# Attention of the second pair of token blocks: two tiles to a TensorE run instead of one

## The chip, the cores and the metric

The kernel runs on one core of one Trainium2 chip. The metric is the time of one launch on the device, in microseconds (us). Five engines work side by side, each through its own queue in order: TensorE (PE, matmuls), VectorE (DVE), ScalarE (ACT), GpSimd (POOL), and SyncE (SP), which only issues DMAs. An engine that needs another's result waits on a semaphore, and everything behind it in its queue waits too.

## The reference, cut to what matters

Attention inside chunks of 64 tokens (8 heads of 64), then a mixture of four experts in which every token goes through every expert, weighted by its normalised probability:

```
scores = q_c @ k_c.T / 8            # per chunk of 64 tokens and head
attn   = exp(scores - max); attn = attn / (sum(attn) + 1e-9)
x      = (attn @ v_c) as 4608 x 512 tokens
p      = domain_probs / (sum + 1e-9)
out    = sum over e of p[:, e] * (relu(x @ w1[e]) @ w2[e])   # 512 -> 1024 -> 512
```

## The kernel before

The 4608 tokens are nine blocks of 512, and a block is four tiles of 128. The first block is worked alone, and the other eight as four pairs. For each pair the weights are gone through in eight passes (four experts, two halves of the hidden units each), numbered n = 8 to 15 for the first pair, 16 to 23 for the second and so on. Products are in split fp32 (a high and a low part, three matmuls for each product of two 128-blocks), and a product of two blocks by two is made by a scheme of seven products instead of eight.

A later pass is 28 **products** of six matmuls 128x512 each, in the written order `WOVEN`: `a1 g1 a2 g2 g6 a5 g5 a6 a3 g7 a7 g4 g3 a4 h1 h2 b1 b5 h6 b6 b3 h5 b7 h7 b2 b4 h4 h3`, counted from 0 (g3 is the 12th, b2 the 24th). The g and h products make hidden units of this pass, the a and b products turn those of the pass before into output. `a` and `b` share the three PSUM banks A1, B1, C1 (class `Outer`), `g` and `h` the banks A0, B0, C0 (class `LaterGroup`). In bank A1 a product is accumulated onto the last one: after a1, a6, a7 and a4, DVE adds the bank's content to an output sum in SBUF (`Outer.add`, L989, rows `acc<-A`). The next matmul into A1 has to wait for that add. So b1 waits for the add after a4, and a1 of the next pass for the add after b4. (In pass 9, where each output sum is begun, that first write is a copy on ACT.)

Beside the matmuls each pass makes the weights' parts for the other passes: half sums (L579, rows `xraw<-xraw`, DVE), high parts on ACT, low parts on POOL.

The attention of the next pair is worked in between. One tile's attention is: scores on PE (32 matmuls of 64x64 in the trace) into PSUM tile `psa`; on DVE the row maxima and their subtraction (`less_max`, L314 and L319); exponentials on ACT (L325); on DVE the **weights** (L328 row sums, L329, L331 inverses, L335 scaling into SBUF, L188 a transpose back into `psa`); on ACT five copies that place the transposed weights (L194, L204); and on PE the values (32 matmuls, L214). A list `at` gives for each position the work that is recorded behind that product; every engine's queue holds it in this recorded order.

For the third and fourth pair `attend_two` handles two tiles to one TensorE run: values of two tiles and scores of the next two, 128 small matmuls together. For the second pair, whose attention stands in passes 9 to 14, `attend` handles one tile to a run: values of tile t and scores of tile t+1, 64 small matmuls. The places are `EARLY` (weights behind the 6th product, placing behind the 9th, run behind the 11th) and `LATE` (17th, 20th, 23rd), and behind each run come the maxima. Passes 10, 12 and 14 have an early run, 11 and 13 an early and a late one, pass 9 the first scores and a late run. The values leave PSUM by ACT and are kept in DRAM (`x_kept`) until the second pair begins.

Of the kernel before, what the change touches and what calls it, by code (L numbers as in the profile page):

```python
# [31 lines left out]
def chunk_attention_moe(ctx: ExitStack, tc: tile.TileContext, qk, v, v0, dp, w1, w2, out):  # L32
# [85 lines left out]
    def a_load(t):  # L118
        s = st[t] = {}
        s["x"] = load.tile([P, 2, 2, HG, C], F32, name="qk_in")  # L120
        nc.sync.dma_start(out=s["x"], in_=qk[t].rearrange("g c d x h s -> (c d) g x h s"))

    def a_load_v(t, odd=(False, True)):
        s = st[t]
        if not odd[0]:
            s["v"] = load.tile([P, 2 * HG, C], F32, name="v_in")
        to, of = (
            a.rearrange("p (g i h) d -> p g i (h d)", g=2, i=2) for a in (s["v"], v[t - NT])
        )
        if not odd[0]:  # L130
            nc.sync.dma_start(out=to[:, :, 0], in_=of[:, :, 0])
        if odd[-1]:
            for half in range(2):
                rows, other = slice(half * C, (half + 1) * C), slice((1 - half) * C, (2 - half) * C)
                nc.sync.dma_start(out=to[rows, :, 1], in_=of[other, :, 1])

    def a_load_after(t):
        if (t + 1 - NT) % (PAIR * NT):
            a_load(t + 1)

    def quarters():

        for g in range(2):
# [8 lines left out]
    def blocks(i):  # L152

        return psa[:, :, i * HG * C : (i + 1) * HG * C].rearrange("p c (j k) -> p c j k", k=C)

    def a_scores(t):
        s = st[t]
        s["sc"] = blocks(0)
        for c, half, slot, head in quarters():
            q, k = (s["x"][of_half(c), head // HG, x, head % HG] for x in range(2))  # L160
            nc.tensor.matmul(s["sc"][of_half(half), c, slot], lhsT=q, rhs=k, start=True, stop=True)  # L161

    def a_less_max(t):
        less_max(st[t]["sc"])

# [4 lines left out]
        a_less_max(t)  # L170
        a_exps(t)

    def a_sums(t):
        z = psa[:, 0, HG * C : HG * C + 2 * HG].rearrange("p (c j) -> p c j", c=2)
        st[t]["r"] = inverse_sums(st[t]["sc"], z)

    def a_scale(t):

        s = st[t]
        s["e"] = att.tile([P, 2, HG, C], F32, name="e")  # L180
        scale(s["e"], s["sc"], s["r"])

    def a_weights(t):
        a_sums(t)
        a_scale(t)

    def a_transpose(t):
        nc.vector.transpose(st[t]["sc"], st[t]["e"])  # L188

    def a_place(t, name="pt", apart=False):  # L190

        s = st[t]
        s["pt"] = att.tile([P, 2, HG, C], F32, name=name)
        nc.scalar.copy(out=s["pt"], in_=s["sc"])  # L194
        if not apart:
            a_place_rest(t)

    def a_place_rest(t):

        s = st[t]  # L200
        for half in range(2):
            for i in range(2):
                here, there = (slice(half * C + k * B, half * C + (k + 1) * B) for k in (i, 1 - i))
                nc.scalar.copy(  # L204
                    out=s["pt"][there, :, :, i * B : (i + 1) * B],
                    in_=s["sc"][here, :, :, (1 - i) * B : (2 - i) * B],
                )

    def a_values(t):

        s = st.pop(t)
        av = blocks(1)
        for c, half, slot, head in quarters():
            nc.tensor.matmul(  # L214
                av[of_half(slot % 2), half, head // 2], lhsT=s["v"][of_half(half), head],
                rhs=s["pt"][of_half(half), c, slot], start=True, stop=True,
            )

    def a_copy(t):
        pair, i = divmod(t - NT, PAIR * NT)  # L220
        if pair == 1:
            tile_x = scratch[0][:, :SUB].rearrange("p (j q) -> p j q", j=NK)
        else:
            tile_x = of_tiles(pair, i, 1)[:, 0]
        to = tile_x.rearrange("p j (c q) -> p c j q", c=2)
        av = blocks(1)
        nc.scalar.copy(out=to[:, :, 0::2], in_=av[:, :, 0::2])
        nc.scalar.copy(out=to[:, :, 1::2], in_=av[:, ::-1, 1::2])
        if pair == 1:
            nc.sync.dma_start(out=x_kept[:, i], in_=tile_x)  # L230

    def x_tiles(pair):
        xraw[pair] = xpool.tile([P, PAIR * NT, NK, P], F32, name="xraw")
# [12 lines left out]
        nc.sync.dma_start(out=to, in_=qk[t].rearrange("g c d x h s -> (c d) g x h s"))  # L248

    def two_load_v(t, i, odd):  # L250
        if i and not odd:
            pair, j = divmod(t - NT, PAIR * NT)
            st[t]["v"] = of_tiles(pair, 7 if j == 7 else 5, 1)[:, 0].rearrange("p j (h d) -> p j h d", h=2)
        elif not odd:
            st[t]["v"] = load.tile([P, NK, 2, C], F32, name="v_in")
        to = st[t]["v"].rearrange("p (g i) h d -> p g i h d", i=2)
        of = v[t - NT].rearrange("p (g i h) d -> p g i h d", g=2, i=2)
        if not odd:
            nc.sync.dma_start(out=to[:, :, 0], in_=of[:, :, 0])
            return  # L260
        for half in range(2):
            rows, other = slice(half * C, (half + 1) * C), slice((1 - half) * C, (2 - half) * C)
            nc.sync.dma_start(out=to[rows, :, 1], in_=of[other, :, 1])
# [17 lines left out]
    def two_next(t, scores, banks=("B1", "C1")):  # L281
# [14 lines left out]
                two_scores(scores + i, i)  # L296
        if av:
            pair, j = divmod(t - NT, PAIR * NT)
            to = of_tiles(pair, j, 2).rearrange("p i j (c q) -> p i j c q", c=2)
            for half in range(2):  # L300
                for odd in range(2):
                    nc.scalar.copy(out=to[:, :, odd::2, half ^ odd], in_=av[half][:, :, odd::2])

    x_kept = dram.tile([P, PAIR * NT, NK, P], F32, name="x_kept")

    def x_back():
        x = x_tiles(1)
# [29 lines left out]
    def attention(pair):  # L337
# [14 lines left out]
        for t in range(first, last, 2):  # L352
# [14 lines left out]
                if i == 0:  # L367
                    loads(t + 1, 1)
            two_next(t, t + 2 if t + 2 < last else None, (None, None))

    def a_next(t, after):

        if t is not None:
            a_values(t)
        if after is not None:
            a_scores(after)

        if t is not None:
            a_copy(t)

    KEYS = {"a11": 0, "a12": 1, "a22": 2, "s1": 3, "s2": 4, "s3": 5, "s4": 6}
    ORDER = (
# [1073 lines left out]
    def plain_pass(n, beside, xs):  # L1461
# [66 lines left out]
        for r, i in ((0, 2), (1, 2), (2, 3), (3, 5), (4, 5)):  # L1528
            add(at, i, lambda r=r: ring_load(0, r, (RINGS[0] + RINGS[1])[r]))
        add(at, 1, lambda: probs_load(n + 1, 0), lambda: probs_load(n + 1, 1))  # L1530
        add(at, 6, lambda: half_load(n + 2, 0), lambda: first_load(1))
        add(at, 6, lambda: ring_load(0, 5, RINGS[1][2]))
        issue(steps[:-1], at, beside, True)
        return steps[-1], w2_do("keep_sums")
# [55 lines left out]
    def probs_load(n, s):  # L1590
# [15 lines left out]
    )  # L1606


    EARLY, LATE = (6, 9, 11), (17, 21, 24)
    TILES = {  # L1610
        1: ((LATE, 0),), 2: ((EARLY, 1),), 3: ((EARLY, 2), (LATE, 3)), 4: ((EARLY, 4),),
        5: ((EARLY, 5), (LATE, 6)), 6: ((EARLY, 7),),
    }
    ALONE = "a1 b1 a2 a5 b5 a6 b6 a3 b7 b2 a7 b3 a4 b4".split()

    def first_load(pair):
        if pair < n_pairs:
            a_load((1 + pair * PAIR) * NT)

    def loads(at, i, t):  # L1620

        for after, f in enumerate((
            lambda: a_load_v(t, (False,)), lambda: a_load_v(t, (True,)), lambda: a_load_after(t),
        )):
            later.append((i + 2 + after, f)) if i + 2 + after >= len(WOVEN) else add(at, i + 2 + after, f)


    later = []

    def attend(at, pair, places, i):  # L1630
        t = (1 + pair * PAIR) * NT + i
        after = t + 1 if i + 1 < PAIR * NT else None
        if i == 0:
            add(at, 13, lambda: a_next(None, t))
            add(at, 14, lambda: a_softmax(t))
            loads(at, 13, t)
        add(at, places[0], lambda: a_weights(t), lambda: a_transpose(t))
        apart = i in (2, 5)
        add(at, places[1] - apart, lambda: a_place(t, apart=apart))
        if apart:  # L1640
            add(at, places[1], lambda: a_place_rest(t))
        add(at, places[2], lambda: a_next(t, after))
        if after:
            add(at, places[2] + 1, lambda: a_softmax(after))
            loads(at, places[2], after)

    def attend_two(at, pair, r):

# [22 lines left out]
    def first_later_pass(n, held, keep_sums):  # L1671
# [19 lines left out]
        add(at, 10, lambda: sc.sum("t4", 0, nc.gpsimd))  # L1691
        add(at, 9, lambda: half_load(n + 1, 1))
        half_sums(at, 0, (4, 4, 5), nc.gpsimd)
        add(at, 6, lambda: make_next(0))
        add(at, 9, lambda: make_next(0))
        add(at, 10, keep_sums)
# [25 lines left out]
    def later_pass(n, ahead, late, held):  # L1722
# [39 lines left out]
        if 0 < pair < n_pairs - 1:  # L1762
            attend_two(at, pair + 1, n % n_pass)
        elif pair == 0:
            for places, i in TILES.get(n % n_pass, ()):
                attend(at, pair + 1, (17, 20, 23) if places == LATE else places, i)
        late = []
        if n + 1 < 2 * n_pass - 1:
            add(at, 5, lambda: half_load(n + 1, 0))
            add(at, 13, lambda: half_load(n + 1, 1, (0,)))  # L1770
            add(at, 19, lambda: half_load(n + 1, 1, (1,)))
            half_sums(at, 0, (11 if n % n_pass in (3, 5) else 15, 21, 21, 21))
        if n_pass < n < 2 * n_pass - 1:
            half_sums(first, 1, (5, 6, 11, 12) if n == n_pass + 1 else (9, 9, 10, 11))
            if n == n_pass + 1:
# [28 lines left out]
        if last_pass and more:  # L1804
# [24 lines left out]
        for i, name in enumerate(WOVEN):  # L1829
# [140 lines left out]
```

## Time and profile before

| what | value |
|---|---|
| median of 3 runs | 1462.17 us (1461.22 to 1462.36) |
| the profiled execution, its own time | 1461.41 us |
| its span, first to last instruction | 1459.6 us |
| PE busy | 1453.5 us (100%) |
| DVE, POOL, ACT busy | 74%, 67%, 43% |
| granted TensorE clock | full in all slices |

PE's matmuls overlap in the trace, so its busy time is not its peak; but it shows that PE hardly ever stands still. The other engines are idle for part of the time, and what they do is free as long as it ends before PE needs it.

### The profile page before, as it was taken

What the parts mean: (1) busy time and instruction counts of PE and PEld (TensorE: products, weight loads), DVE (VectorE), ACT (ScalarE), POOL (GpSimd) and SP (SyncE); (2) the same over time, 40 slices, a digit from 0 to 9 for tenths busy, and PEclk for the clock granted to TensorE, in tenths of its full rate; (3) what the DMA queues carried; (4) which work ended last, traced back from release to release, by engine and by line L of the source; (5) the groups of instructions that cost most, each with busy time, mean ns of one, the idle gap of its engine ahead of it and who ended that gap; (6) DMA issues with size and microseconds to landing.
All of it is one profiled execution on the core that took longest, in us unless ns stands there. A gap on an engine that the chain in (4) does not pass through costs nothing.

```text
span 1459.6 us, 23405 instructions
## 1 busy us (share of the span) xinstructions
PE 1453.5 (100%) x8574; PEld 1199.5 (82%) x8574; DVE 1078.2 (74%) x1500; ACT 623.8 (43%) x1169; POOL 975.1 (67%) x728
## 2 busy tenths in 40 slices
PE   9999999999999999999999999999999999999998
PEld 7888888888888888888888888888888888888887
DVE  6566758888887986777767977777668856666666
ACT  5556545445454444443433435444334343223332
POOL 5878888887888775555557655555557655555555
PEclk9999999999999999999999999999999999999999
DMA  9899787878779689665565798676566685556555
GB/s 320 302 347 321 260 320 265 271 239 272 235 253 345 212 258 293 228 224 203 190 209 191 231 229 276 219 244 198 194 200 201 202 255 200 198 199 200 204 189 156
DMA packets 198994, 348.51 MB, mean 239 GB/s; under 512 B 70224, under 2 KB 109408, under 8 KB 198496
## 3 DMA queue, kind: packets, MB, share of 16 engines
q1 hardware_dynamic: 198880, 347.02, 72.4%
q8 instruction: 68, 1.11, 0.3%
q14 instruction: 46, 0.38, 0.1%
HBM read 275.59 MB, written 71.38 MB: 238 GB/s over the span
## 4 chain that ended last, share of the span: by engine, by line
PE 99%; DVE 0%; issue 0%; ACT 0%
PE A L764 51%; PE C L764 28%; PE B L764 16%; PE psa L270 1%; PE B L289 1%; PE psa L214 0%; PE psa L161 0%; PE C L1264 0%; PE C L289 0%; PE A L1264 0%; PE C L1299 0%; PE psa L1153 0%; PE B L1162 0%; PE B L1172 0%; PE A L289 0%; PE psa L1220 0%
## 5 line engine op out<-in xcount | busy, mean ns | idle before, releaser
L942 POOL TENSOR_TENSOR hf<-wraw,hf 128x512 fp32r<-128x512 f32 x384 | 507.2, 1338 | 227.1 <-ACT hf L939 225.8
L764 PE MATMUL A<-hf,wf 128*128 128x512 f32 x1536 | 391.4, 390 | 0.0
L764 PE MATMUL A<-xh,wf 128*128 128x512 f32 (+1 forms) x1120 | 387.1, 389 | 0.0
L939 ACT CAST hf<-wraw 128x512 fp32r<-128x512 f32 x384 | 233.4, 622 | 288.4 <-DVE wraw L933 99.7
L764 PEld LDWEIGHTS A<-hf,wf 128*128 128x128 f32 x1536 | 286.7, 188 | 61.3 <-DVE acc L989 1.8
L764 PEld LDWEIGHTS A<-xh,wf 128*128 128x128 f32 x1120 | 210.0, 188 | 43.9 <-issue 0.3
L827 ACT COPY s<-A 128x512 f32<-128x512 f32 x192 | 112.7, 587 | 291.3 <-PE A L764 290.9
L764 PE MATMUL A<-xl,wf 128*128 128x512 f32 (+1 forms) x560 | 217.5, 388 | 0.0
L989 DVE TENSOR_TENSOR acc<-A,acc 128x512 f32<-128x512 f32 x232 | 157.8, 680 | 65.2 <-PE A L764 64.8
L764 PE MATMUL C<-xh,wf 128*128 128x512 f32 (+1 forms) x584 | 201.7, 389 | 0.0
L764 PE MATMUL C<-hf,wf 128*128 128x512 f32 x768 | 194.7, 389 | 0.0
L764 PEld LDWEIGHTS C<-hf,wf 128*128 128x128 f32 x768 | 144.2, 188 | 29.9
L764 PEld LDWEIGHTS C<-xh,wf 128*128 128x128 f32 x584 | 109.5, 188 | 22.7
L933 POOL TENSOR_TENSOR wf<-wraw,wf 128x512 f32<-128x512 f32 x31 | 40.1, 1294 | 128.5 <-DVE wf L927 127.4
L764 PEld LDWEIGHTS A<-xl,wf 128*128 128x128 f32 x560 | 105.2, 188 | 21.7
L942 POOL TENSOR_TENSOR hf<-wf,hf 128x512 fp32r<-128x512 f32 x64 | 90.8, 1418 | 47.3 <-ACT hf L939 47.3
L764 PE MATMUL B<-xh,wf 128*128 128x512 f32 (+1 forms) x344 | 115.5, 384 | 0.0
L989 DVE TENSOR_TENSOR acc<-C,acc 128x512 f32<-128x512 f32 x120 | 82.6, 689 | 43.2 <-PE C L764 39.0
L764 PE MATMUL C<-xl,wf 128*128 128x512 f32 (+1 forms) x292 | 113.3, 388 | 0.0
L933 DVE TENSOR_TENSOR wraw<-wf,wraw 128x512 f32<-128x512 f32 x64 | 95.6, 1493 | 5.6 <-POOL hf L942 4.5
L764 PE MATMUL B<-hf,wf 128*128 128x512 f32 x384 | 97.9, 390 | 0.0
L933 POOL TENSOR_TENSOR wraw<-wraw 128x512 f32<-128x512 f32 x63 | 91.7, 1456 | 0.0
(259 smaller groups left out, 1980.4 us busy)
## 6 DMA issues: line engine op xcount, KB each, us to landing
wf<-w SPq DMA_DIRECT2D x402, 512.0 KB, 4.2
w<-wf SPq DMA_DIRECT2D x46, 512.0 KB, 5.3
w<-hf SPq DMA_DIRECT2D x28, 512.0 KB, 6.6
w<-hf SPq DMA_DIRECT2D x42, 256.0 KB, 5.1
qk_in<-in_qk SPq DMA_DIRECT2D x20, 512.0 KB, 6.2
wf<-in_w SPq DMA_DIRECT2D x19, 512.0 KB, 6.3
xraw<-in_qk SPq DMA_DIRECT2D x14, 512.0 KB, 7.3
ws<-p_t SPq DMA_DIRECT2D x24, 256.0 KB, 4.1
```

Of the source, the lines that this page charges most:

```text
L270: nc.tensor.matmul(s["sc"][of_half(half), c, slot], lhsT=q, rhs=k, start=True, stop=True)
L289: nc.tensor.matmul(av[half][of_half(slot % 2), i, head // 2], lhsT=s["v"][of_half(half), head // 2, head % 2], rhs=s["pt"][of_half(half), ...
L764: nc.tensor.matmul(out, lhsT=lhs(k, a), rhs=rhs(k, b), start=first and i == 0, stop=last and i == len(parts) - 1, skip_group_check=not (fi ...
L827: nc.scalar.copy(out=t, in_=self.a)
L933: (eng or nc.vector).tensor_tensor(out=self.values[place, k], in0=self.values[a, k], in1=self.values[b, k], op=op)
L939: nc.scalar.copy(out=self.part(name, 0)[:, k], in_=self.values[name, k])
L942: (eng or nc.gpsimd).tensor_tensor(out=self.part(name, 1)[:, k], in0=self.values[name, k], in1=self.part(name, 0)[:, k].bitcast(F32), op=A ...
L989: nc.vector.tensor_tensor(out=acc[key], in0=src, in1=acc[key], op=ALU.add)
```

## The change

The second pair's attention goes two tiles to a run, as the later pairs' does, at places of its own:

- q and k of two tiles are loaded together into `hf3`, the buffer that holds T4's parts of the hidden units at other times (`both_load`, behind the 26th product of passes 9 to 11, and behind the 3rd step of pass 7 for the first two tiles).
- The first scores are a run in pass 8; then passes 10, 11 and 12 have one run each of 128 small matmuls, behind the product at place 5 (the sixth), and pass 13 a last run of values.
- In passes 10 to 12 the maxima of the first tile stand behind place 6 (the seventh product) and those of the second behind place 17; the weights behind places 12 and 24 (the 13th and 25th); the placing behind 15 and 27. In pass 9 the weights stand behind 17 and 24.
- The values use the banks B1 and C0 (g5's); so in passes 10 to 13 a6 and g5 change places. The sums of the weights use bank B1.
- The output tiles leave through `qk_in`, two to a DMA. The first half sum stands behind place 15 in all passes (in passes 11 and 13 it stood behind 11).

```diff
+    def both_load(t):
+        both = hf_tile(3, (2, 2, 2, HG, C), F32)
+        for i in range(2):
+            st[t + i] = {"x": both[:, i]}
+            nc.sync.dma_start(out=both[:, i], in_=qk[t + i].rearrange("g c d x h s -> (c d) g x h s"))
...
-            to = of_tiles(pair, j, 2).rearrange("p i j (c q) -> p i j c q", c=2)
+            x = load.tile([P, 2, NK, P], F32, name="qk_in") if pair == 1 else of_tiles(pair, j, 2)
+            to = x.rearrange("p i j (c q) -> p i j c q", c=2)
...
+            if pair == 1:
+                nc.sync.dma_start(out=x_kept[:, j : j + 2], in_=x)
...
-    EARLY, LATE = (6, 9, 11), (17, 21, 24)
...
+    def attend_second(at, n):
+        t0, r = (1 + PAIR) * NT, n - n_pass - 1
+        t = t0 + 2 * max(r, 0)
+        if r < 0:
+            add(at, 2, lambda: two_next(None, t))
+            for i in range(2):
+                add(at, 3, lambda i=i: a_less_max(t + i))
+                add(at, 5 + i, lambda i=i: a_exps(t + i))
+            return
+        if r > 4:
+            return
+        if r:
+            add(at, 5, lambda: two_next(t - 2, t if r < 4 else None, ("B1", "C0")))
+        if r == 4:
+            return
+        if r:
+            add(at, 6, lambda: a_softmax(t))
+            add(at, 17, lambda: a_softmax(t + 1))
+        first, second = ((12, 15), (24, 27)) if r else ((17, 20), (24, 27))
+        add(at, first[0], lambda: two_weights(t))
+        add(at, first[1], lambda: a_place(t))
+        add(at, second[0], lambda: two_weights(t + 1))
+        add(at, second[1], lambda: a_place(t + 1, "e"))
...
+        if r < 3:
+            add(at, 26, lambda: both_load(t + 2))
...
-            for places, i in TILES.get(n % n_pass, ()):
-                attend(at, pair + 1, (17, 20, 23) if places == LATE else places, i)
+            attend_second(at, n)
...
-            half_sums(at, 0, (11 if n % n_pass in (3, 5) else 15, 21, 21, 21))
+            half_sums(at, 0, (15, 21, 21, 21))
...
+        order = list(WOVEN)
+        if n_pass + 2 <= n <= n_pass + 5:
+            order[6:8] = order[7:5:-1]
```

Two places of DVE's queue show what the table of places does. The first is behind g3 (place 12) in pass 10; `A` and `C` are PSUM banks, `s` a kept partial product, `m` the maxima, `z` the inverse sums. Before:

```order
L927 SCALAR_TENSOR_TENSOR wraw<-A_3156,s_2979 128x512
L579 TENSOR_TENSOR xraw<-xraw 128x256
L962 TENSOR_TENSOR C_3214<-C_3214,s_3199 128x512
L927 SCALAR_TENSOR_TENSOR wf_3338<-C_3214,ws 128x512
L314 TENSOR_REDUCE m_3341<-psa 128x8
L319 TENSOR_TENSOR psa<-psa,m_3341 128x2x256
L989 TENSOR_TENSOR acc_2881<-A_3147,acc_2881 128x512
L962 TENSOR_TENSOR B_3370<-B_3370,s_3362 128x512
```

And the same place now (the line numbers are those of the changed file):

```order
L861 SCALAR_TENSOR_TENSOR wraw<-A_3151,s_3002 128x512
L513 TENSOR_TENSOR xraw<-xraw 128x256
L896 TENSOR_TENSOR C_3297<-C_3297,s_3194 128x512
L861 SCALAR_TENSOR_TENSOR wf_3368<-C_3297,ws 128x512
L277 TENSOR_REDUCE B_3371<-psa 128x8
L278 TENSOR_SCALAR B_3371<-B_3371 128x8
L280 RECIPROCAL z_3374<-B_3371 128x8
L284 TENSOR_TENSOR e<-psa,z_3374 128x512
L155 STREAM_TRANSPOSE psa<-e 128x2x256
L923 TENSOR_TENSOR acc_2922<-A_3142,acc_2922 128x512
L896 TENSOR_TENSOR B_3400<-B_3400,s_3394 128x512
```

In front of the add after a4 (the row `acc<-A`) there stood the two instructions of the maxima, and now there stand the five of the weights. The second place is behind b2 (place 24) of the same pass. Before:

```order
L962 TENSOR_TENSOR B_3475<-C_3446,s_3476 128x512
L927 SCALAR_TENSOR_TENSOR wraw<-B_3475,ws 128x512
L989 TENSOR_TENSOR acc_2939<-B_3484,acc_2939 128x512
L989 TENSOR_TENSOR acc_3113<-A_3383,acc_3113 128x512
L927 SCALAR_TENSOR_TENSOR wraw<-A_3355,s_2979 128x512
```

Now:

```order
L896 TENSOR_TENSOR B_3513<-C_3484,s_3514 128x512
L861 SCALAR_TENSOR_TENSOR wraw<-B_3513,ws 128x512
L923 TENSOR_TENSOR acc_2962<-B_3522,acc_2962 128x512
L277 TENSOR_REDUCE B_3535<-psa 128x8
L278 TENSOR_SCALAR B_3535<-B_3535 128x8
L280 RECIPROCAL z_3538<-B_3535 128x8
L284 TENSOR_TENSOR e<-psa,z_3538 128x512
L155 STREAM_TRANSPOSE psa<-e 128x2x256
L923 TENSOR_TENSOR acc_3105<-A_3417,acc_3105 128x512
```

Between the add after b2 (`acc<-B`) and the add after b4 (`acc<-A`) nothing stood in pass 10 and the two instructions of the maxima in pass 11; now the five of the weights stand there in passes 10, 11 and 12.

## Rows read from the trace of the kernel before

**Rows 1.** The page: span, busy time of each engine, the last chain.

```profile
span 1459.6 us, 23405 instructions
...
PE 1453.5 (100%) x8574; PEld 1199.5 (82%) x8574; DVE 1078.2 (74%) x1500; ACT 623.8 (43%) x1169; POOL 975.1 (67%) x728
...
PE 99%; DVE 0%; issue 0%; ACT 0%
```

**Rows 2.** The waits of PE, whole span: who for whom, total, times, longest.

```profile
PE C L1299 <- DVE s L1293: 1.2, 1, 1.2
PE B L1234 <- DVE e L335: 0.6, 1, 0.6
PE B L1899 <- DVE acc L1891: 0.3, 1, 0.3
```

**Rows 3.** Order in time, PE: start, length, instruction; passes' starts and runs.

```profile
240.01 0.39 PE L764 MATMUL A<-hf,wf 128*128 128x512 f32 x1
240.33 0.74 PE L161 MATMUL psa<-qk_in 64*64 64x64 f32 x32
241.00 0.50 PE L764 MATMUL A<-xh,wf 128*128 128x512 f32 x1
...
261.58 0.62 PE L764 MATMUL A<-hf,wf 128*128 128x512 f32 x2
...
301.07 1.52 PE L764 MATMUL A<-hf,wf 128*128 128x512 f32 x6
...
341.94 0.84 PE L764 MATMUL A<-hf,wf 128*128 128x512 f32 x3
...
595.10 0.27 PE L289 MATMUL B<-pt,v_in 64*64 64x64 f32 x1
...
635.51 0.27 PE L289 MATMUL B<-pt,v_in 64*64 64x64 f32 x1
```

**Rows 4.** Stretch of pass 10: length, then PE, PEld, DVE, ACT, POOL busy.

```profile
261.58:301.07 39.49, 39.49 (x233) 32.54 (x232) 34.37 (x48) 18.34 (x36) 31.82 (x24) 1.00 0.85 264
```

**Rows 5.** Order in time, DVE: the weights of one tile and what follows.

```profile
270.79 0.69 DVE L328 TENSOR_REDUCE psa<-psa 128x8 f32<-128x512 f32 x1
...
273.33 0.67 DVE L989 TENSOR_TENSOR acc<-A,acc 128x512 f32<-128x512 f32 x1
```

**Rows 6.** Order in time around place 12 of pass 10, DVE and b1.

```profile
276.00 0.70 DVE L962 TENSOR_TENSOR B<-C,s 128x512 f32<-128x512 f32 x1 [1.21 <-ACT s L827]
...
279.73 0.41 DVE L579 TENSOR_TENSOR xraw<-xraw 128x256 f32<-128x256 f32 x1
280.87 0.70 DVE L962 TENSOR_TENSOR C<-C,s 128x512 f32<-128x512 f32 x1 [0.73 <-PE C L764]
...
282.28 0.68 DVE L314 TENSOR_REDUCE m<-psa 128x8 f32<-128x512 f32 x1
...
283.60 0.68 DVE L989 TENSOR_TENSOR acc<-A,acc 128x512 f32<-128x512 f32 x1
...
284.75 0.62 PE L764 MATMUL A<-hf,wf 128*128 128x512 f32 x2
```

**Rows 7.** Order in time around place 24 of pass 10, ACT and DVE.

```profile
295.83 0.59 ACT L827 COPY s<-A 128x512 f32<-128x512 f32 x1 [0.68 <-PE A L764]
...
292.36 3.31 DVE L579 TENSOR_TENSOR xraw<-xraw 128x256 f32<-128x256 f32 x3
...
297.30 0.69 DVE L962 TENSOR_TENSOR B<-C,s 128x512 f32<-128x512 f32 x1
...
298.63 0.68 DVE L989 TENSOR_TENSOR acc<-B,acc 128x512 f32<-128x512 f32 x1
299.23 0.68 DVE L989 TENSOR_TENSOR acc<-A,acc 128x512 f32<-128x512 f32 x1
```

**Rows 8.** The page's DMA issues; ACT's copies out of a later pair's run.

```profile
qk_in<-in_qk SPq DMA_DIRECT2D x20, 512.0 KB, 6.2
...
596.84 0.67 ACT L302 COPY xraw<-C 128x256 f32<-128x256 f32 x2
```

More of the change, by code (lines that the diff above doesn't have):

```diff
@@ L121, in a_load @@
         nc.sync.dma_start(out=s["x"], in_=qk[t].rearrange("g c d x h s -> (c d) g x h s"))
[L123 to L139, printed above, removed]
     def quarters():
@@ L154, in blocks @@
         return psa[:, :, i * HG * C : (i + 1) * HG * C].rearrange("p c (j k) -> p c j k", k=C)
[L156 to L161, printed above, removed]
     def a_less_max(t):
@@ L171, in a_softmax @@
         a_exps(t)
-    def a_sums(t):
-        z = psa[:, 0, HG * C : HG * C + 2 * HG].rearrange("p (c j) -> p c j", c=2)
-        st[t]["r"] = inverse_sums(st[t]["sc"], z)
     def a_scale(t):
@@ L181, in a_scale, with a_place @@
         scale(s["e"], s["sc"], s["r"])
-    def a_weights(t):
-        a_sums(t)
-        a_scale(t)
     def a_transpose(t):
         nc.vector.transpose(st[t]["sc"], st[t]["e"])
-    def a_place(t, name="pt", apart=False):
+    def a_place(t, name="pt"):
         s = st[t]
@@ L194, in a_place @@
         nc.scalar.copy(out=s["pt"], in_=s["sc"])
[L195 to L200, printed above, removed]
         for half in range(2):
@@ L207, in a_place_rest @@
                 )
[L209 to L230, printed above, removed]
     def x_tiles(pair):
@@ L250, in two_load_v @@
     def two_load_v(t, i, odd):
-        if i and not odd:
-            pair, j = divmod(t - NT, PAIR * NT)
+        pair, j = divmod(t - NT, PAIR * NT)
+        if i and pair == 1:
+            if not odd:
+                st[t]["v"] = scratch[0][:, :SUB].rearrange("p (j h d) -> p j h d", j=NK, h=2)
+        elif i and not odd:
             st[t]["v"] = of_tiles(pair, 7 if j == 7 else 5, 1)[:, 0].rearrange("p j (h d) -> p j h d", h=2)
@@ L369, in attention @@
             two_next(t, t + 2 if t + 2 < last else None, (None, None))
[L371 to L379, printed above, removed]
     KEYS = {"a11": 0, "a12": 1, "a22": 2, "s1": 3, "s2": 4, "s3": 5, "s4": 6}
@@ L1530, in plain_pass @@
         add(at, 1, lambda: probs_load(n + 1, 0), lambda: probs_load(n + 1, 1))
-        add(at, 6, lambda: half_load(n + 2, 0), lambda: first_load(1))
+        add(at, 3, lambda: both_load((1 + PAIR) * NT))
+        add(at, 6, lambda: half_load(n + 2, 0))
         add(at, 6, lambda: ring_load(0, 5, RINGS[1][2]))
@@ L1606, in chunk_attention_moe @@
     )
-    EARLY, LATE = (6, 9, 11), (17, 21, 24)
[L1610 to L1613, printed above, removed]
     ALONE = "a1 b1 a2 a5 b5 a6 b6 a3 b7 b2 a7 b3 a4 b4".split()
@@ L1618, in first_load @@
             a_load((1 + pair * PAIR) * NT)
[L1620 to L1625, printed above, removed]
-    later = []
[L1630 to L1645, printed above, removed]
+    later = []
+    def attend_second(at, n):
[21 more added lines that the diff above has]
+        add(at, second[1], lambda: a_place(t + 1, "e"))
+        for i in range(2):
+            for odd in range(2):
+                add(at, (7 if r else 14) + 2 * i + odd, lambda i=i, odd=odd: two_load_v(t + i, i, odd))
+        if r < 3:
+            add(at, 26, lambda: both_load(t + 2))
     def attend_two(at, pair, r):
@@ L1764, in later_pass @@
         elif pair == 0:
-            for places, i in TILES.get(n % n_pass, ()):
-                attend(at, pair + 1, (17, 20, 23) if places == LATE else places, i)
+            attend_second(at, n)
         late = []
@@ L1828, in later_pass @@
                 late[:0] = [(0, x("lo", "t1")), (2, lambda: sc.sum("t4", 0, nc.gpsimd))]
-        for i, name in enumerate(WOVEN):
+        order = list(WOVEN)
+        if n_pass + 2 <= n <= n_pass + 5:
+            order[6:8] = order[7:5:-1]
+        for i, name in enumerate(order):
             getattr(steps[name[0]], f"p{name[1]}")()
```

## Prediction

> **What bounds the kernel now.** I read the page first: PE is busy for 1453.5 of 1459.6 us, and the chain that ended last is PE for 99% [rows 1]. Then PE's waits: three, at the two ends of the program, 2.1 us together [rows 2]. So no engine but PE sets the time, and a change can act in two ways only: it gives PE less or more to do, or it makes another engine late for PE. The first is counted from PE's own starts, the second from DVE's order in time at the places where the change puts work in front of something that PE waits for.
>
> The reader is to see in the third view what one run costs: pass 10 lasts from 261.58 to 301.07, that is 39.49 us with one run in it, and pass 11 from 301.07 to 341.94, 40.87 us with two [rows 3]. One run of one tile therefore costs 1.38 us all told, and a pass without one 38.11 us, or 1.36 for each of 28 products and 0.227 for each of 168 matmuls. In the later pairs the starts of two runs lie 40.41 us apart (595.10 to 635.51) with one run of two tiles in between [rows 3]: 2.30 us. In the fourth view DVE is busy for 34.37 of pass 10's 39.49 us with one tile's attention in it [rows 4]. In the sixth and seventh, DVE's adds out of bank A1, for which b1 and the next a1 wait, end only 0.47 and 1.16 us before PE comes (below). That is the room that the change has.
>
> **PE's own work.** The matmuls stay the same in number; what changes is how often PE turns from large to small and back. Before: seven runs of 1.38, and one of scores and one of values alone. From the matmul before the scores (240.01) to the one behind them (241.00) pass 0.99 us [rows 3], 0.76 more than 0.227, and a little is lost behind it, so I take 0.85 for each (with 0.76 the sum falls by 0.2). Sum 7 x 1.38 + 2 x 0.85 = 11.4. After: three runs of 2.30, and at the ends 64 small matmuls each, as many as in a one-tile run, 1.38: 6.9 + 2.8 = 9.7. Gain 1.7 us.
>
> **The weights behind place 12.** In passes 10 to 12 the five DVE instructions of the weights now stand in front of the add after a4. From the start of the first to the start of what follows pass 2.54 us (270.79 to 273.33) [rows 5]. In pass 10 the maxima stood there: from 282.28 to 283.60, 1.32 us, and the add then ran to 284.28, with b1 at 284.75 [rows 6]. With 2.54 in that place the add starts at 284.82 and ends at 285.50, and b1 comes 0.75 late. That holds if DVE reaches the place as early against PE as before. It doesn't: the run in front of g3 (1.38) is gone from there, so PE is there 1.38 sooner, while DVE works without a pause from 276.00, when it got what it waited for from ACT, to 280.14 (279.73 + 0.41), and then stood 0.73 us waiting for g3 [rows 6]. Those 0.73 are used up, and 0.65 are missing. So b1 stalls 0.75 + 0.65 = 1.40 us in each pass, and 0.75 if the work before gets shorter by as much. I take 1.40, since that is what the rows of this very place give.
>
> **The weights behind place 24.** In pass 10 the add after b2 starts at 298.63 and the one after b4 at 299.23, ending at 299.91, with a1 at 301.07 [rows 3, 7]: 1.16 us of room for 2.54 us of weights. The add ends at 302.45, and a1 of the next pass stalls 1.38 us. Here too there is a floor: DVE was late at this place. The kept product that the chain begins with was ready at 296.42 (ACT's copy, 295.83 + 0.59), but DVE came to it at 297.30, because three half sums before had taken 3.31 us [rows 7]. Without any lateness the chain to the add after b2 and on would start at 296.42, and 1.93 us of it (297.30 to 299.23), 2.54 of weights and 0.68 of the add lead to 301.57: a stall of 0.50 even then. I take 1.38.
>
> In pass 11 two instructions of maxima stood here already, but with a run before them, at 23, that gave DVE 1.38 us; both go. In pass 9 the weights also stand behind 24, but there the write after b4 is ACT's copy, so nothing of DVE's is late; pass 13 has no weights. So three passes pay at each place.
>
> **What else moves, at no cost.** The maxima behind place 6 stand where weights stood (1.22 less), those behind 17 add 1.32 us; DVE's load in a pass with two tiles is 34.37 + 3.86 = 38.2 us of some 40.4, so DVE is nearly full, which is why I give it no chance to catch up by itself. q and k of the next two tiles (512 KB each, 6.2 us to landing [rows 8]) wait for b4 to leave `hf3` and are needed behind place 5 of the next pass, eight products or 10.9 us later; what the cover would cost if gone is in the rivals. SP's queue gets them behind DMAs that wait for PE at about the same place. T4's parts, written behind places 6 and 7, wait for the scores to leave `hf3`, but the first product that reads them is a4, seven products on (9.5 us). g5's bank C0 must be emptied by ACT first; in the later pairs those copies end at 597.51 (596.84 + 0.67), 2.4 us after the run's start at 595.10 [rows 3, 8], which is about the run's own length, and a6 (1.36) now stands between. The four placing copies more behind 15 and 27 change only ACT's order, and ACT is half idle [rows 4]. The first half sum's place changes two passes that lose more than that to the weights.
>
> **The sum.** 3 x (1.40 + 1.38) - 1.7 = +6.6 us on the profiled execution's 1461.41, that is 1468.1. The median of the runs shown is 0.76 us above that execution, so 1468.8. By the floors it is 3 x (0.75 + 0.50) - 1.7 = +2.05, 1464.2.
>
> **Rivals.**
> 1. *DVE isn't late.* The work taken out at places 6 to 11 lets DVE arrive at both places without backlog, and only the floors are paid: 1464.2. For it: 1.22 us less behind place 6, and a stall at place 12 gives DVE time for place 24. Against it: the 1.21 us pause before 276.00 [rows 6] was for ACT, so what is saved before it is lost in it. Chance 0.14.
> 2. *The half sums get dearer.* A half sum took 0.41 us at 279.73, but three took 3.31 at 292.36 [rows 6, 7], 1.10 each, while POOL was busy for 31.82 of pass 10's 39.49 us [rows 4]. Four of them stand before place 12. If two in a pass pay the difference of 0.69, it is 3 x 1.4 = 4.1 us more: 1472.9. Nothing in the rows says which will meet a POOL instruction once PE's run no longer stands there. Chance 0.10.
> The Trainium skill's page "SBUF — State Buffer" (section "SBUF: two separate sides") says that a DVE instruction with two SBUF inputs and a GpSimd instruction share a pair of ports as an exclusive lock, so that the later one waits out the whole of the other. The trace agrees: 0.41 against 1.10 us for the same half sum. By that rule all four could pay, 1477 in all, while the weights, with their operands in PSUM, would stay at 2.54.
> 3. *Nothing is late, and PE keeps the 1.7 us*: 1460.5, faster. The place is the add after a4 and after b4; it decides for this if the weights' five instructions take at most 1.79 us at place 12 and 1.16 at place 24 in DVE's queue. The only thing for it is that their sums now go to bank B1 and not to `psa`. Against it stand 2.54 us [rows 5] and the order itself, in which the add has no way past them. Chance 0.03.
> 4. *q and k come late.* Two DMAs of 512 KB at once beside the weights' loads, landing 2 us beyond the 10.9: 3 x 2 = 6 us more if it happened in each pass, 1472 if only in half of them. One such load takes 6.2 us, so both together would have to take nearly twice as long. Chance 0.05.
>
> **How the numbers follow.** A measurement of this kernel can tell about 0.2%, 2.9 us, from no change: same is 1459.3 to 1465.1. My forecast, both stalls at about the size of the rows, has 0.68, with a range of its own from 1466 to 1471. Rival 1 spreads from 1463.5 to 1466, three quarters of it within "same". So slower is 0.68 + 0.03 + 0.10 + 0.05 = 0.86, same 0.11 + 0.02 = 0.13, faster 0.01. The range from 1464.0 to 1473.0 takes in the floor and most of rivals 2 and 4.
>
> **What would show it.** Right: PE's waits gain six of about 0.7 to 1.8 us on DVE's rows `acc<-A`, in pairs, at b1 and at the first product of passes 11, 12 and 13; passes 10 to 12 last 43 us each; DVE's rows stand without a pause from the weights to the add. Runs of 128 small matmuls cost 2.3 us. The forecast is wrong if PE shows no waits there, if they name POOL, ACT or a DMA instead, or if the second pair's passes 9 to 13 together aren't longer than before.

## The result, and the profile after

The changed kernel takes 1478.55 us (median of 4 runs, 1477.98 to 1481.18) where the kernel before takes 1461.7: 1.0119 times as long, with a 95% interval of 1.0101 to 1.0136. It is slower by 16.9 us; the forecast was 6.6, and 1473 the upper end of its range. The profiled execution grew by 16.5 us. In all profiles of the changed file L698 is the matmul of the products, L923 the add into `acc`, L513 the half sums, L277 to L155 the weights, L263 and L268 the maxima.

The page after, the same lines as in [rows 1]: span, busy time, the last chain.

```profile
span 1476.1 us, 23391 instructions
...
PE 1456.3 (99%) x8574; PEld 1198.6 (81%) x8574; DVE 1082.4 (73%) x1500; ACT 624.5 (42%) x1169; POOL 975.8 (66%) x728
...
PE 91%; DVE 4%; POOL 2%; DMA 2%; issue 1%; SPq 1%; ACT 0%; POOLq 0%; DVEq 0%
```

PE has as many instructions as before, and the chain that ended last has lost 8% of PE to others. PE's waits show where (who for whom, total, times, longest; compare [rows 2]):

```profile
PE A L698 <- DVE acc L923: 11.3, 9, 1.9
...
PE C L1106 <- DMA ws<-in_v: 0.6, 1, 0.6
...
PE A L698 <- POOL wf L531: 0.5, 1, 0.5
```

There are nine new waits for DVE's adds. PE's order in time shows those of pass 10 (b1, b4 and the next pass's a1), and that passes 11 and 12 repeat them:

```profile
289.03 0.73 PE L698 MATMUL A<-hf,wf 128*128 128x512 f32 x2 [1.71 <-DVE acc L923]
...
301.72 0.50 PE L698 MATMUL A<-hf,wf 128*128 128x512 f32 x1 [0.16 <-DVE acc L923]
307.99 0.96 PE L698 MATMUL A<-hf,wf 128*128 128x512 f32 x3 [1.87 <-DVE acc L923]
334.22 0.50 PE L698 MATMUL A<-hf,wf 128*128 128x512 f32 x1 [1.72 <-DVE acc L923]
...
353.19 0.50 PE L698 MATMUL A<-hf,wf 128*128 128x512 f32 x1 [1.89 <-DVE acc L923]
```

A bracket holds idle time, and the modelled end of the matmul before hides part of the stall. So I take stalls from start to start, less the ordinary 0.227 us between two starts: b1 2.10 to 2.11, that is 1.88 us each; b4 0.55, that is 0.33; a1 2.26 to 2.28, that is 2.04. From 307.99 to 353.19 the pass lasts 45.2 us, where 43 had been forecast.

DVE's order around place 12 of pass 10, to be held against [rows 6] (a row ends later than the next one starts by some 0.08 us, so lengths are taken from start to start):

```profile
279.81 0.70 DVE L896 TENSOR_TENSOR B<-C,s 128x512 f32<-128x512 f32 x1 [1.29 <-ACT s L761]
...
282.60 0.41 DVE L513 TENSOR_TENSOR xraw<-xraw 128x256 f32<-128x256 f32 x1
...
283.54 0.92 DVE L513 TENSOR_TENSOR xraw<-xraw 128x256 f32<-128x256 f32 x1
284.38 0.69 DVE L896 TENSOR_TENSOR C<-C,s 128x512 f32<-128x512 f32 x1
...
285.77 0.69 DVE L277 TENSOR_REDUCE B<-psa 128x8 f32<-128x512 f32 x1
...
288.31 0.67 DVE L923 TENSOR_TENSOR acc<-A,acc 128x512 f32<-128x512 f32 x1
```

From 279.81 DVE has no pause left; the 0.73 us that it stood in front of `C<-C,s` before are gone. The weights take 2.54 (285.77 to 288.31), to the hundredth what was forecast. New is the half sum at 283.54: 0.92, where the one of that place took 0.41. GpSimd's instruction beside it, in the kernel before and then now:

```profile
280.53 1.29 POOL L597 TENSOR_TENSOR wf<-xraw,wf 128x512 fp32r<-128x512 f32 x1 [3.51 <-ACT wf L596]
```

```profile
282.82 1.35 POOL L531 TENSOR_TENSOR wf<-xraw,wf 128x512 fp32r<-128x512 f32 x1 [1.89 <-ACT wf L530]
```

Before, it began after the half sum (279.73) had ended; now it begins 0.72 us ahead of it. And around place 24, to be held against [rows 7], DVE and then GpSimd:

```profile
296.77 4.30 DVE L513 TENSOR_TENSOR xraw<-xraw 128x256 f32<-128x256 f32 x3
300.99 0.68 DVE L923 TENSOR_TENSOR acc<-A,acc 128x512 f32<-128x512 f32 x1
...
304.72 0.70 DVE L277 TENSOR_REDUCE B<-psa 128x8 f32<-128x512 f32 x1
...
307.26 0.67 DVE L923 TENSOR_TENSOR acc<-A,acc 128x512 f32<-128x512 f32 x1
```

```profile
296.63 2.73 POOL L876 TENSOR_TENSOR hf<-wraw,hf 128x512 fp32r<-128x512 f32 x2
299.32 1.47 POOL L531 TENSOR_TENSOR wf<-xraw,wf 128x512 fp32r<-128x512 f32 x1
```

Three half sums took 4.30 us where they had taken 3.31, and GpSimd works all the while. They begin 0.14 us behind the start of GpSimd's pair of instructions, and began 1.12 behind it in the kernel before (292.36):

```profile
291.24 2.72 POOL L942 TENSOR_TENSOR hf<-wraw,hf 128x512 fp32r<-128x512 f32 x2
```

Over the whole trace of the changed kernel, the 15 half sums that meet no GpSimd instruction take 0.41 to 0.43 us each, the six during which one begins 0.41 to 0.42, and the 24 that begin while one is running 0.41 to 1.51, 1.20 in the mean. The add behind the three (300.99) is the one for which b4 now waits.

One thing more is in this profile. Stretches behind the third a1 stall: length, then PE, PEld, DVE, ACT, POOL busy, granted clock, DMA share, GB/s.

```profile
398.40:400.00 1.60, 1.58 (x7) 1.30 (x8) 1.56 (x3) 1.00 (x2) 0.31 (x1) 0.96 0.04 15
400.00:403.50 3.50, 3.50 (x10) 2.74 (x9) 3.43 (x4) 2.84 (x8) 3.50 (x3) 0.53 0.00 0
403.50:405.00 1.50, 1.50 (x8) 1.20 (x8) 1.50 (x3) 0.91 (x3) 1.50 (x2) 1.00 0.02 5
```

For 3.4 us PE has its lower clock, 1.2 GHz, and eight matmuls stand 0.43 apart instead of 0.227: 1.6 us.

The 16.5 us come out as follows: b1 3 x 1.88 = 5.64; a1 6.13; b4 0.98; the matmul behind each of the nine waits 0.11 longer, 1.0; GpSimd's parts late for PE in passes 9 and 10, 0.20 + 0.63 + 0.22 behind them = 1.05; half clock 1.6; a later start, 1.24 (the first product run is at 53.20 instead of 51.96, with a wait for a DMA of `in_v` that the other kernels' profiles show at 0 to 0.8); less 1.7 for fewer runs. Sum 15.9; of the other 0.6, some 0.3 lies in gaps of a few ns in passes 8 to 13, and 0.26 behind the last product.

### The profile page after: what moved, and what is told of

Read it like the earlier page. It is cut to its first block, busy times and chain, and to the rows that moved or that the text cites. A ratio compares the mean times of both kernels' runs of the same rounds, so it can differ in the third digit from the quotient of the medians.

```text
span 1476.1 us, 23391 instructions
## 1 busy us (share of the span) xinstructions
PE 1456.3 (99%) x8574; PEld 1198.6 (81%) x8574; DVE 1082.4 (73%) x1500; ACT 624.5 (42%) x1169; POOL 975.8 (66%) x728
## 4 chain that ended last, share of the span: by engine, by line
PE 91%; DVE 4%; POOL 2%; DMA 2%; issue 1%; SPq 1%; ACT 0%; POOLq 0%; DVEq 0%
PE A L698 48%; PE C L698 26%; PE B L698 15%; POOL hf L876 1%; DVE xraw L513 1%; PE psa L209 1%; DVE acc L923 1%; PE B L228 1%; DMA ws<-in_v 1%; DMA qk_in<-in_v 1%; DMA v_in<-in_v 0%; POOL wraw L867 0%; POOL wf L531 0%; PE C L228 0%; DVE e L284 0%
## 5 line engine op out<-in xcount | busy, mean ns | idle before, releaser
L698 PE MATMUL A<-hf,wf 128*128 128x512 f32 x1536 | 393.0, 391 | 11.3 <-DVE acc L923 11.3
L698 PE MATMUL A<-xh,wf 128*128 128x512 f32 (+1 forms) x1120 | 388.0, 390 | 0.5 <-POOL wf L531 0.5
L698 PEld LDWEIGHTS A<-hf,wf 128*128 128x128 f32 x1536 | 285.5, 188 | 75.9 <-DVE acc L923 16.7
L698 PEld LDWEIGHTS A<-xh,wf 128*128 128x128 f32 x1120 | 210.2, 188 | 45.2 <-POOL wf L531 1.7
L698 PE MATMUL A<-xl,wf 128*128 128x512 f32 (+1 forms) x560 | 217.9, 389 | 0.0
L923 DVE TENSOR_TENSOR acc<-A,acc 128x512 f32<-128x512 f32 x232 | 157.9, 681 | 77.9 <-PE A L698 77.2
L698 PE MATMUL C<-xh,wf 128*128 128x512 f32 (+1 forms) x584 | 201.2, 388 | 0.0
L698 PE MATMUL C<-hf,wf 128*128 128x512 f32 x768 | 194.7, 389 | 0.0
L698 PEld LDWEIGHTS C<-hf,wf 128*128 128x128 f32 x768 | 144.2, 188 | 30.0
L698 PEld LDWEIGHTS C<-xh,wf 128*128 128x128 f32 x584 | 109.5, 188 | 22.7
L698 PEld LDWEIGHTS A<-xl,wf 128*128 128x128 f32 x560 | 105.5, 188 | 22.0
L923 DVE TENSOR_TENSOR acc<-C,acc 128x512 f32<-128x512 f32 x120 | 82.7, 689 | 51.1 <-PE C L698 47.7
L698 PE MATMUL B<-xh,wf 128*128 128x512 f32 (+1 forms) x344 | 115.4, 384 | 0.0
L698 PE MATMUL C<-xl,wf 128*128 128x512 f32 (+1 forms) x292 | 113.2, 388 | 0.0
L698 PE MATMUL B<-hf,wf 128*128 128x512 f32 x384 | 98.1, 390 | 0.0
L867 DVE TENSOR_TENSOR wraw<-wf,wraw 128x512 f32<-128x512 f32 x64 | 92.3, 1443 | 5.5 <-POOL hf L876 4.4
```

What stands on the lines that cost most here:

```text
L698: nc.tensor.matmul(out, lhsT=lhs(k, a), rhs=rhs(k, b), start=first and i == 0, stop=last and i == len(parts) - 1, skip_group_check=not (fi ...
L867: (eng or nc.vector).tensor_tensor(out=self.values[place, k], in0=self.values[a, k], in1=self.values[b, k], op=op)
L923: nc.vector.tensor_tensor(out=acc[key], in0=src, in1=acc[key], op=ALU.add)
```

## The experiments

All but the last are the changed kernel with an edit of the places, each run beside the kernel before on the same chip. **C** below is the theory that I came to: a stall comes of all the DVE work in front of the add since DVE's last pause, half sums included, and a half sum costs two to three times as much where a GpSimd instruction is already running (1.20 us in the mean for 0.41, above).

### Each tile's weights behind its add

```
-        first, second = ((12, 15), (24, 27)) if r else ((17, 20), (24, 27))
+        first, second = ((12, 15), (25, 27)) if r else ((17, 20), (24, 27))   # e1
+        first, second = ((13, 16), (24, 27)) if r else ((17, 20), (24, 27))   # e2
+        first, second = ((13, 16), (25, 27)) if r else ((17, 20), (24, 27))   # e3
```

Expected of the first: 

> The second tile's weights stand behind place 25 (behind b4's add) instead of 24; all else as in the changed kernel. Theory A (each stall belongs to the weights in front of its own add, and the places don't pass lateness on): the three waits at the first product of the next pass (2.04 us each in the changed kernel) and the slower matmuls behind them (about 0.15 each) are gone, the ones at b1 (1.88) and b4 (0.33) stay: 1478.5 - 3 x 2.2 = 1472, and 1470.3 if the stretch at half clock behind the third of them goes too. Theory B (DVE is simply full, so the lateness moves on to the next add): another wait of 1 to 2 us per pass appears at g1, a2 or b1, and the time stays above 1476.

Of the second: 

> The first tile's weights stand behind place 13 (behind a4's add) and are placed behind 16; the second tile's as in the changed kernel. Theory A: the three waits at b1 (1.88 us each) and what is lost behind them (0.15) go, those at b4 and at the next pass's first product stay at 0.33 and 2.04: 1478.5 - 3 x 2.0 = 1472.4; the stretch at half clock stays. Theory B: PE now comes 1.9 us sooner to places 21 to 25 while DVE has as much to do, so the waits at b4 and at the first product grow by about that, and the time stays above 1476.

Of both: 

> Both moves together: first weights behind place 13, second behind 25. Theory A: only the three waits at b4 (0.33 us, the three half sums in front of b7's add) are left: 1478.5 - 3 x (1.88 + 2.04 + 0.3) = 1465.8, and 1464 if the stretch at half clock goes too; with the 1.7 us of fewer runs this is 2 to 3 us above what a kernel without any wait would take. Theory B: DVE is full and new waits of 1 us and more come up at other adds: above 1470.

Measured: 1475.85 (ratio 1.0097, 1.0082 to 1.0112), 1473.45 (1.0084, 1.0067 to 1.0101) and 1472.77 (1.0078, 1.0063 to 1.0093). With the weights behind b4's add a1 no longer waits, but the next product does, and one after it:

```profile
307.54 0.67 DVE L861 SCALAR_TENSOR_TENSOR wraw<-A,s 128x512 f32<-128x512 f32 x1
...
308.26 0.50 PE L698 MATMUL A<-xh,wf 128*128 128x512 f32 x1 [1.00 <-DVE wraw L861]
...
313.67 0.73 PE L698 MATMUL A<-xh,wf 128*128 128x512 f32 x2 [0.58 <-POOL wf L531]
```

What stands behind the weights now is the scaled value that leaves bank A for g1. By starts the two cost 1.16 and 0.74 us in place of 2.04. With the first weights behind a4's add, b1's 1.88 is gone, b5 waits 0.41, and b4 waits 1.04 instead of 0.33; a1 stays at 2.0:

```profile
290.77 1.65 PE L698 MATMUL A<-hf,wf 128*128 128x512 f32 x6 [0.25 <-DVE acc L923]
300.15 1.20 PE L698 MATMUL A<-hf,wf 128*128 128x512 f32 x4 [0.88 <-DVE acc L923]
```

So theory A of these expectations (lateness stays in its place) falls: in the second run its time, 1472.4, is the nearer one, but b4's wait should have stayed at 0.33. B is half right, for a part of the lateness moves on: to the next thing that PE needs from DVE, smaller by the pauses in between. None of the three profiles has a stretch at half clock.

### The half sums away from GpSimd

```
-            half_sums(at, 0, (15, 21, 21, 21))
+            half_sums(at, 0, (15, 17, 17, 17) if n_pass < n else (15, 21, 21, 21))
```

> The weights stay where the changed kernel has them; the three half sums of passes 10 and later in the second pair stand behind place 17 instead of 21, where GpSimd is idle for some us. Theory C (what the forecast lacked at place 24 is the half sums beside GpSimd, 4.30 us for three that take 1.23 alone): the wait at b4 goes, that at the next pass's first product falls from 2.04 to about 0.5, b1's stays at 1.88: 1478.5 - 3 x (0.33 + 1.5) = 1473.0. Rival D (the weights alone make that stall, and the half sums only fill time in which DVE would wait anyway): the half sums get short but the wait at the first product stays above 1.4: 1476 or more.

Measured: 1472.04 (1.0071, 1.0056 to 1.0086). DVE's order and GpSimd's in pass 10:

```profile
294.55 1.09 DVE L513 TENSOR_TENSOR xraw<-xraw 128x256 f32<-128x256 f32 x3
...
299.42 0.69 DVE L923 TENSOR_TENSOR acc<-A,acc 128x512 f32<-128x512 f32 x1 [1.78 <-PE A L698]
300.03 1.67 DVE L867 TENSOR_TENSOR wraw<-wraw 128x512 f32<-128x512 f32 x1
```

```profile
291.94 2.54 POOL L876 TENSOR_TENSOR hf<-wraw,hf 128x512 fp32r<-128x512 f32 x2 [2.93 <-ACT hf L873]
295.92 1.48 POOL L531 TENSOR_TENSOR wf<-xraw,wf 128x512 fp32r<-128x512 f32 x1 [1.45 <-ACT wf L530]
```

The same three instructions take 1.09 us instead of 4.30, in GpSimd's pause between 294.48 and 295.92. The wait at b4 is gone, DVE even stands 1.78 us in front of that add, a1's wait falls from 2.04 to 0.91, and b1's stays at 1.88. Rival D is out: 1.1 of a1's 2.04 came from the half sums. (The 0.91 is more than the expected 0.5, since the sum in `wraw` at 300.03 now meets GpSimd: 1.67 for the 1.17 that it took in the changed kernel. Without these 0.50 it would be 0.41, near the floor of 0.50 that the forecast had for this place.) The edit applies in pass 9 too, and early in pass 10 there are then two waits, 0.58 and 0.75, in place of one of 0.63.

### The second tile without a stall

```
-        first, second = ((12, 15), (24, 27)) if r else ((17, 20), (24, 27))
+        first, second = ((12, 15), (21, 24)) if r else ((17, 20), (24, 27))
-            half_sums(at, 0, (15, 21, 21, 21))
+            half_sums(at, 0, (15, 17, 17, 17) if n_pass + 1 < n else (15, 21, 21, 21))
```

> Against the changed kernel, in passes 10 to 12: the three half sums stand behind place 17 instead of 21, and the second tile's weights (2.54 us) take the place they leave, behind 21 instead of 24; pass 9 and the first tile's weights stay. In the run with the half sums alone at 17, DVE waited 1.78 us for PE just behind place 21 and the wait at the next pass's first product was 0.91. Theory C: 2.54 us of weights there make the add before b4 end about 0.8 us later than in that run, still before PE needs it, and add nothing behind b2: only the three waits at b1 (1.88 us each, and 0.15 behind each) are left: 1478.5 - 3 x (0.33 + 2.04 + 0.3) = 1470.5, less 1.7 if the stretch at half clock of that execution goes: 1468.8. Rival (the maxima's exponentials aren't ready at 21, or the weights make b4's add late): a wait of about 1 us at b4: 1473 or more.

Measured: 1468.81 (1.0050, 1.0036 to 1.0063), as forecast. The waits of the products for DVE are down to b1's three, 1.88 each by starts:

```profile
PE A L698 <- DVE acc L923: 5.2, 3, 1.7
```

### One half sum out of the way of b1

```
-            half_sums(first, 1, (5, 6, 11, 12) if n == n_pass + 1 else (9, 9, 10, 11))
+            half_sums(first, 1, (5, 6, 11, 12) if n == n_pass + 1 else (9, 9, 10, 14))
```

At place 14 this half sum reads one of its inputs when the next load has already overwritten it, so these passes use other data; the instructions are the same. The edit moves it in passes 13 and 14 too, where no weights stand.

> The changed kernel with one half sum of passes 10 to 12 moved from place 11, in front of the first tile's weights, to place 14, behind a4's add; it took 0.92 us there beside a GpSimd instruction (0.41 where none runs), 0.84 from its start to the next. Theory C (at b1 DVE works without a pause, and all that stands in front of a4's add is in the stall): the three waits at b1 fall from 1.88 to about 1.04, those at b4 and the first products stay within 0.1: 1478.0 - 2.5 = 1475.5. Rival (the weights alone set this stall, DVE would wait for the ACT copy or for g3 anyway): b1's wait stays above 1.6, the time above 1477.

Measured: 1476.26 (1473.96 to 1479.43; 1.0108, 1.0091 to 1.0125). The forecast for b1 holds:

```profile
288.04 1.66 PE L698 MATMUL A<-hf,wf 128*128 128x512 f32 x6 [0.88 <-DVE acc L923]
...
292.65 0.73 PE L698 MATMUL A<-hf,wf 128*128 128x512 f32 x2 [0.22 <-DVE acc L923]
```

The stall at b1 is 1.04 in pass 10 (1.05 and 1.04 in the next two), 0.84 less than 1.88. So the whole of this half sum was in the stall. The other waits did not stay as expected: b4's is gone in all three passes, b5 waits 0.38 in pass 10, and the next a1's wait is 2.07 behind pass 10 and 1.51 behind passes 11 and 12.

### The first tile as well

```
-        first, second = ((12, 15), (24, 27)) if r else ((17, 20), (24, 27))
+        first, second = ((13, 16), (21, 24)) if r else ((17, 20), (24, 27))
-            half_sums(at, 0, (15, 21, 21, 21))
+            half_sums(at, 0, (17, 17, 17, 17) if n_pass + 1 < n else (15, 21, 21, 21))
```

> As the last one, and the first tile's weights stand behind place 13 (behind a4's add), placed behind 16, and the half sum of place 15 is at 17 as well, since with weights behind 13 it stood in the way of b5 (0.41 us). Theory C: passes 10 to 12 have no wait of more than 0.3 us, so what is left against the kernel before is its 1.7 us for fewer runs less one or two waits in passes 8 and 9 (0.2 to 1.3 us): 1460 to 1462, the same as before. Rival (DVE is full with two tiles per pass, 38.2 of 40.4 us, and lateness comes up elsewhere): 3 x 0.5 to 3 x 1.5 us of other waits: 1463 to 1467.

Measured: 1469.13 (1.0055, 1.0041 to 1.0068), above both ranges and so on the rival's side: a new wait of 1.85 us in each pass. DVE's row names it:

```profile
292.35 0.69 DVE L263 TENSOR_REDUCE m<-psa 128x8 f32<-128x512 f32 x1 [1.50 <-ACT pt L165]
```

The second tile's maxima stood waiting for ACT to have placed the first tile. That is a wait in the order, not DVE's load. The next two kernels take it out:

```
-            add(at, 17, lambda: a_softmax(t + 1))
+            add(at, 8, lambda: a_softmax(t + 1))          # e8
+            add(at, 8, lambda: a_less_max(t + 1))         # e9
+            add(at, 11, lambda: a_exps(t + 1))
```

> As the run with all moved, and the second tile's maxima stand behind place 8 instead of 17. In that run they stood 1.50 us waiting for ACT's placing of the first tile, and a new wait of 1.85 us came up on PE two products later; behind place 8 DVE has pauses of 0.72 and 1.29 us for 1.32 us of maxima. Theory C (lateness comes only of what stands in front of an add when DVE has no pause there): passes 10 to 12 have no wait over 0.3 us, 1469.1 - 3 x (1.85 + 0.2 + 0.15) = 1462.5, and down to 1460.5 without the waits of passes 8, 9 and 13. Rival (DVE is full): the wait comes up at another add, 1 to 2 us per pass: 1465 to 1468.

> As the run with early maxima, but the second tile's exponentials stand behind place 11 of ACT's order instead of behind 8, where they stood in front of the kept copy for which PE waited 1.24 us in each of passes 10 to 12. Theory C: that wait and the slower matmuls behind it go: 1468.2 - 3 x 1.4 = 1464.0; what is left against the kernel before less 1.7 (1459.8) are waits of passes 8, 9 and 13 and 0.2 us in each of three passes. Rival (there is always another add, DVE being full): a wait of 1 us or more in each pass stays: 1467 or more.

The first: 1468.16 (1.0046, 1.0032 to 1.0061), at the rival's upper end. The wait at the later place is gone, and one on ACT has come; ACT's order and PE's row show why:

```profile
280.36 0.58 ACT L274 ACTIVATE psa<-psa 128x512 f32<-128x512 f32 x1 [1.62 <-DVE psa L268]
280.85 0.61 ACT L530 CAST wf<-xraw 128x512 fp32r<-128x512 f32 x1
281.36 0.59 ACT L761 COPY s<-A 128x512 f32<-128x512 f32 x1
```

```profile
282.00 0.50 PE L698 MATMUL A<-xh,wf 128*128 128x512 f32 x1 [1.08 <-ACT s L761]
```

The exponentials waited for DVE's maxima, and the kept copy, which PE needs, stood behind them. With the exponentials behind place 11: 1463.2 (11 runs; 1.0010, 1.0001 to 1.0019), against 1464.0 expected. From 276 us to the end of pass 12 no gap between two starts is then over 0.34, and what is left of PE's waits is of passes 8 to 10 and 13 (three of the rows):

```profile
PE B L698 <- POOL hf L876: 0.5, 1, 0.5
PE A L698 <- POOL wf L531: 0.5, 1, 0.5
...
PE A L698 <- POOL hf L876: 0.2, 1, 0.2
```

So "DVE is full" isn't the reason: with the same work on every engine, 15 of the 17 us were a matter of order. One more edit moved pass 9's weights from 17 and 24 to 14 and 18.

> As the last one, and in pass 9 the weights stand behind 14 and 18 instead of 17 and 24 (placed behind 17 and 21). Behind 24 of pass 9 they delay a scaled value, so that GpSimd's part of g6 was 0.63 us late for PE in pass 10 in each run. Theory C: that goes, with 0.11 behind it: 0.7 us below the last kernel, near 1463. Rival: the weights at 14 and 18 stand in front of pass 9's own adds and new waits come up there, so that it is 1 us or more above the last kernel.

Measured: 1463.72 (1.0013, 1.0004 to 1.0022): the wait of 0.63 fell to 0.18, and one of 0.89 came in pass 9. It lies between what the theory and the rival had, and nothing is gained; no version that I ran beats the kernel before.

### The changed kernel again

> The changed kernel once more, nothing edited. What it tells: of the 16.5 us by which its profiled execution was longer, 1.7 lay in a stretch of 3.4 us at half clock behind the last of the six large waits, and 1.2 in a later start. If these belong to the kernel, the profile shows them again; if they belong to that one execution, this profile is about 3 us shorter (span near 1473) and the waits at b1, b4 and the first products are the same to 0.1 us.

Measured: 1477.6 (1.0109, 1.0095 to 1.0123). The nine waits are the same to 0.03 us, the first product run starts at 52.47, and the half clock is there again, now behind the second a1 stall (353.77):

```profile
353.70:354.70 1.00, 0.93 (x4) 0.80 (x5) 1.00 (x3) 0.36 (x1) 0.00 (x0) 1.00 0.81 164
354.70:358.60 3.90, 3.90 (x12) 3.05 (x11) 3.80 (x5) 2.91 (x8) 3.56 (x3) 0.56 0.79 283
```

Most of the later start belongs to the one execution, then (0.51 of 1.24 is left). The half clock came in both profiles of this kernel, though not at one place. GpSimd's parts cost PE 2 us in passes 8 to 10 here, 1.05 in the first profile; that too changes from one execution to the next.

## Why the prediction was right in its direction and wrong in its size

- **The gain of fewer runs** was right. A run of two tiles, the values and scores of 128 small matmuls, goes from 271.32 to 273.40, and costs 2.17 beside one ordinary step and 0.11 in the matmul behind it; forecast 2.30. By starts, all runs of the second pair took 11.2 us before and take 9.5 now, 1.8 less; forecast 1.7.

```profile
272.79 0.69 PE L209 MATMUL psa<-hf 64*64 64x64 f32 x32
273.40 0.96 PE L698 MATMUL A<-hf,wf 128*128 128x512 f32 x3
```

- **The mechanism was right**: waits on `acc<-A`, at b1 and at the first product of the next pass, in passes 10 to 12, with the weights at 2.54 us. That q and k come in time held: no product waits for them.
- **The step that failed: "What else moves, at no cost", and with it the two terms of 1.40 and 1.38.** They measured 1.88, and 2.04 with 0.33 more at b4. I priced all that stands in front of the weights by what it took in the kernel before, half sums at 0.41 at place 12 and 3.31 for three at place 21. But when PE's run is moved, ACT's and GpSimd's work shifts against DVE's, and the half sums meet GpSimd's instructions otherwise.
  - At place 12, ACT's cast that GpSimd waits for stood behind copies out of that run, 3.82 us behind `B<-C,s` (279.82); without them it comes 2.31 behind it (282.12), so that GpSimd begins ahead of the half sum. 7.34 us pass from `B<-C,s` to b1's turn, and DVE needs 288.31 + 0.67 - 279.81 = 9.17, with 0.05 until PE starts: 1.88, or 0.48 more than forecast; the half sum has 0.43 of it, from start to start.
  - At place 21 the three sums began 0.98 us sooner against GpSimd's pair and took 4.30 - 3.31 = 0.99 more, as much as b4's 0.33 and the 0.66 by which a1's 2.04 is above the forecast.
  - Together that is 1.42 a pass, 4.3 us. The run with the half sums at 17 shows this for place 21; for place 12 it rests on the rows, since no run took GpSimd's instruction away from that half sum.
- **Rival 2 was the right mechanism, and its size is luck.** I had it at 4.1 us (1472.9) and gave it 0.10, because "nothing in the rows says which will meet a POOL instruction". It priced two of the four sums in front of place 12 at 0.69 more each; one of them cost 0.43, and the three at place 21, which it left as they were, 0.99. The rows did show that those three met GpSimd already, and that GpSimd was busy for 31.82 of 39.49 us [rows 4]; 0.10 was less than they bear.
- The Trainium skill's page "SBUF — State Buffer" (section "SBUF: two separate sides") says that a DVE instruction with two SBUF inputs and a GpSimd instruction that reads SBUF take a shared pair of ports in turn, and that the one that starts first keeps it for its whole length. The trace agrees: the half sum at 282.60, which began before GpSimd's instruction (282.82), took 0.41, and the one at 283.54, behind that start, 0.92; in the run with the half sums at 17 three took 1.09 against 4.30.
- **b4's wait for b7's add was not foreseen**, for I followed only the add behind the weights and not the one in front of them.
- **Outside the sum** were 0.11 us behind each wait (1.0), GpSimd's lateness in passes 8 to 10 (1.0 to 2) and the half clock (1.6). The stalls came to 12.75 instead of 8.34, 4.4 more; 6.6 + 4.4 + 1.0 + 1.05 + 1.6 = 14.7 us belong to the change in that execution, and 1.2 to the later start.
- **Rivals 1 and 3** (floors; nothing late) are out by the stalls themselves. Rival 1 counted on a stall at place 12 to give DVE time for place 24. The run with only the first weights moved, behind place 13, shows that it did so at b4 alone: without b1's stall, b4's grew by 0.71 and a1's did not change.

What stays open: why the clock falls behind one a1 stall in the changed kernel and not behind the others. It isn't the length of that stall alone: in the first profile the stalls at 353.19 and 398.42 are both 2.05 us and the clock falls behind the second only, and the kernel with the first weights behind 13 has three of 2.0 us and keeps the full clock.

## What to carry to other kernels

When work is put in front of an instruction for which another engine waits, price the whole queue back to the last pause of the engine that does the work, not the new work alone: what stands in between keeps its length only if its neighbours on the other engines stay beside it. For an instruction whose length in the trace varies with its company, take both lengths as likely, and ask which company the change will give it. Work that is moved behind the add, as here, can bring the stall back at the next result that PE needs, smaller by the pauses between; it went for good only where the work landed in a pause of its queue and nothing else in that queue had to wait there.

## What the runs showed of the hardware that was not expected

- The lower clock for 3.4 us in the midst of a kernel whose PE is busy for 99%, 1.1 to 1.5 us behind the end of a wait of 2.05 in both profiles of the changed kernel, and 0.5 us behind the a1 stall of 2.07 (307.19) in the one with a half sum at place 14:

```profile
307.10:308.10 1.00, 0.91 (x3) 0.75 (x4) 1.00 (x3) 0.34 (x1) 0.00 (x0) 0.78 0.91 193
308.10:311.30 3.20, 3.20 (x9) 2.49 (x9) 3.10 (x4) 2.74 (x7) 2.84 (x2) 0.54 0.68 262
```

- Behind each wait and each run of small matmuls one step, from the first matmul to the second, takes 0.335 to 0.341 us instead of 0.227, however long the wait was (0.33 to 2.05).
- The same DVE instruction on 128 x 256 values in SBUF took 0.41 to 0.43 us where GpSimd did nothing beside it or began later, and up to 1.51 us where a GpSimd instruction was already running.
